# Sparse attention with a feed-forward layer: tile addresses on multiples of 512 bytes, and one place instead of two per attention group

## The chip, the cores and the metric

The kernel runs on one core of a Trainium2 chip. The metric is device time in microseconds (us) of one execution, as the median of several runs. TensorE (PE in the profile) does the matrix products, VectorE (DVE) and ScalarE (ACT) the elementwise work, GpSimd (POOL) a little at the start, and SyncE (SP) issues the transfers.

## What is computed

Attention with two sparse masks over 8 batches of 576 tokens and 8 heads of 64, and a two-layer feed-forward network over the 4608 tokens that it gives. The reference, cut to what matters:

```python
def _attn_ref(q, k, v):                 # q, k, v: (8, 8, 576, 64), float32
    scores = scale * np.matmul(q, k.transpose(0, 1, 3, 2))
    mask_local = (rel >= 0) & (rel < 32)                      # heads 0 to 3
    mask_strided = (rel >= 0) & (pos_k % 32 == pos_q % 32)    # heads 4 to 7
    scores = np.where(masks, scores, -1e9)
    attn = np.exp(scores - np.max(scores, axis=-1, keepdims=True))
    attn = attn / (np.sum(attn, axis=-1, keepdims=True) + 1e-09)
    return np.matmul(attn, v)

def _moe_ref(x, w_in, w_out):           # x: (4608, 512), w_in: (512, 2048)
    h = x @ w_in
    return (h * (1.0 / (1.0 + np.exp(-h)))) @ w_out
```

## The kernel before

**Attention.** A batch is cut into six groups (`GROUPS`, line 77): groups 0 to 2 hold tiles of the local mask, groups 3 to 5 tiles of the strided one. A group `c` of all 48 goes through five steps on TensorE, and each is followed by work elsewhere:

- `scores` (line 348): small products of q and k into a PSUM bank; `peak` (line 358) then masks and finds the maxima on VectorE, and ScalarE takes the exponentials (line 376); `total` (line 391) finishes the sums on VectorE;
- `turn` (line 402): three or four 128x128 transposes of the exponentials (`sm`), and a copy to `pt` on ScalarE (line 410);
- `values` (line 412): small products with v (line 418 for a local group, 426 for a strided one), followed by `share` on VectorE (local) or `sorted` on ScalarE (strided);
- `back` (line 452), for local groups alone: three transposes of `xq` (line 456), and `done` copies them to `xb` on ScalarE.

**Feed-forward.** The tokens are cut into nine blocks of 512, and d_ff into 16 chunks of 128. `hidden` (line 488) is a stretch of 12 matmuls, 128x128 stationary and 512 columns moving: the weights stand in the array, `xhi` or `xlo` moves. `silu` makes `ghi` and `glo` of it on ScalarE and VectorE (lines 498, 502, 510, 514). `output` (line 534) is again a stretch of 12 wide matmuls: `ghi` or `glo` stands in the array and the second layer's weights move. It works one chunk behind, so the order on TensorE is hidden(fc), output(fc - 1), hidden(fc + 1), and so on: two stretches a chunk, 32 a block. Both layers keep a high and a low part of every float32 value, hence three products per term.

**Weights of the second layer.** Chunks 0 to 6 and the low part of 7 and 8 have tiles of their own. The rest is kept in tiles that the start no longer needs (`lent`, line 175): the high parts of chunks 7 and 8 in `kbd2`, the high parts of chunks 9 to 11 in `vbd2`, their low parts in `zeros`, chunks 12 to 15 in `stage0` to `stage3`. All of them are read by TensorE as the moving operand.

**Order.** Block 0 is arranged by a small planner (`Steps`, lines 97 to 159). From block 1 on TensorE's order is written out by hand (lines 745 to 780); the order on the other engines follows from a scheduler, while dependencies decide the waits. While block k runs, the attention of batch k + 1 is done between the stretches: `plan` (line 746) gives each group two places, counted in half chunks. At the first stand `back` of the group before and `values` of the group; three half chunks later `turn` of the next group, `scores` of the one after that and `total`. The PSUM ring `ps` has four banks, which `hidden` and all attention steps share.

Of the kernel before, what the change touches and what calls it, by code (L numbers as in the profile page):

```python
# [13 lines left out]
F32 = mybir.dt.float32  # L14
# [9 lines left out]
B, H, S, D = 8, 8, 576, 64  # L24
# [4 lines left out]
P = 128  # L29
# [3 lines left out]
NFC = DFF // P  # L33
# [11 lines left out]
VT = 12  # L45
KBUFS = 2
VBUFS = 2
# [115 lines left out]
def sparse_attention_ffn(ctx: ExitStack, tc: tile.TileContext, kqt, vt, w_in, w_out, out):  # L163
    nc = tc.nc
    const = ctx.enter_context(tc.tile_pool(name="const", bufs=1))
    io = ctx.enter_context(tc.tile_pool(name="io", bufs=2))
    xp = ctx.enter_context(tc.tile_pool(name="xp", bufs=2))
    att = ctx.enter_context(tc.tile_pool(name="att", bufs=2))
# [10 lines left out]

    kbds = [const.tile([P, 3, QW], F32, name=f"kbd{i}") for i in range(KBUFS + 1)]
    vbds = [const.tile([P, 2, VT * D], F32, name=f"vbd{i}") for i in range(VBUFS + 1)]
    zeros = const.tile([P, VT * D], F32, name="zeros")
    ident = const.tile([P, P], F32, name="ident")

# [12 lines left out]
    vbds = [vbd.rearrange("p h (t d) -> p h t d", d=D) for vbd in vbds]  # L199
# [7 lines left out]
    def keep(m, p0, rows, shape, steps, base, channel):  # L207
        part = m[p0 : p0 + rows, : math.prod(shape)]
        nc.gpsimd.affine_select(
            out=part, in_=part, pattern=[[s, c] for s, c in zip(steps, shape)],  # L210
            base=base, channel_multiplier=channel, compare_op=ALU.is_ge, fill=NEG,
        )
# [15 lines left out]
    for t in range(P // KW):  # L228
        keep(m, t * KW, KW, [4, NJ], [-NJ, -1], 0, 1)
        keep(m, t * KW, KW, [4, NJ], [NJ, 0], NJ - 1, -1)  # L230
    masks[False, ()] = m


    cuts = ((0, NFC), (0, 7, 9, 12, 14, NFC))
# [91 lines left out]
    class Attention:  # L326
# [21 lines left out]
        def scores(self):  # L348
            g, kbd = self.g, self.kbd
            self.pss = self.bank("pss")  # L350
            s_ps = self.pss.rearrange("p (c h k) -> p c h k", h=2, k=KW)
            for t, c, rows in self.tiles:
                nc.tensor.matmul(  # L353
                    s_ps[rows, c], kbd[:, 1, g.q0[t] : g.q0[t] + g.rows],
                    kbd[:, 0:3:2, g.k0[t] : g.k0[t] + KW], start=True, stop=True,
                )

        def peak(self):
            g = self.g
            s_ps = self.pss.rearrange("p (c h k) -> p c h k", h=2, k=KW)  # L360
            self.sm = att.tile([P, 512], F32, name="sm", bufs=3)
            self.s_sb = s_sb = self.sm.rearrange("p (c k h) -> p c h k", h=2, k=KW)
            self.nmax = nmax = att.tile([P, 4, 2], F32, name="nmax", bufs=4)
            self.rsum = rsum = att.tile([P, 4, 2], F32, name="rsum", bufs=4)
            self.inv = rsum[:, : g.n].unsqueeze(3).broadcast_to([P, g.n, 2, KW])
            for c in range(g.n):
                for h in range(2):

                    nc.vector.tensor_tensor_reduce(  # L369
                        out=s_sb[:, c, h], in0=s_ps[:, c, h],  # L370
                        in1=masks[g.local, g.starts[c]][:, :KW],
                        scale=-SCALE, scalar=BIG, op0=ALU.add, op1=ALU.min,
                        accum_out=nmax[:, c, h : h + 1],
                    )
                    if not self.quick:
                        nc.scalar.activation(  # L376
                            out=s_sb[:, c, h], in_=s_sb[:, c, h], func=AF.Exp,
                            bias=nmax[:, c, h : h + 1], scale=-1.0,
                            accum_out=rsum[:, c, h : h + 1],
                        )  # L380
# [10 lines left out]
        def total(self):  # L391
            rsum, s_sb = self.rsum[:, : self.g.n], self.s_sb[:, : self.g.n]
            if self.quick:
                nc.vector.tensor_reduce(out=rsum, in_=s_sb, op=ALU.add, axis=mybir.AxisListType.X)
            nc.vector.tensor_scalar_add(rsum, rsum, 1e-9)
            nc.vector.reciprocal(rsum, rsum)
# [5 lines left out]
        def turn(self):  # L402
            self.psp = self.bank("psp")
            for c in range(self.g.n):
                at = slice(c * P, (c + 1) * P)
                nc.tensor.transpose(self.psp[:, at], self.sm[:, at], ident)  # L406
# [5 lines left out]
        def values(self):  # L412
            g, pt, vbd = self.g, self.pt, self.vbd
            self.pso = pso = self.bank("pso")
            if g.local:
                o_ps = pso.rearrange("p (c h d) -> p c h d", h=2, d=D)
                for t, c, rows in self.tiles:
                    nc.tensor.matmul(  # L418
                        o_ps[rows, c], pt[:, c * P + rows.start : c * P + rows.stop], vbd[:, :, t],
                        start=True, stop=True,  # L420
                    )
                return
            for t, c, rows in self.tiles:
                p0 = c * P + rows.start
                for h in range(2):
                    nc.tensor.matmul(  # L426
                        pso[h * D : (h + 1) * D, t * SEQ : (t + 1) * SEQ], vbd[:, h, t],
                        pt[:, p0 : p0 + SEQ], start=True, stop=True,
                    )
# [22 lines left out]
        def back(self):  # L452
            self.psx = self.bank("psp")
            for c in range(self.g.n):
                at = slice(c * P, (c + 1) * P)
                nc.tensor.transpose(self.psx[:, at], self.xq[:, at], ident)  # L456
# [6 lines left out]
    def new_x():  # L463
        return [ffn.tile([P, NP, T], F32R, name=n, bufs=1) for n in ("xhi", "xlo")]
# [9 lines left out]
    def x_high(k, x, cc, engine="ACT"):  # L474
        for src, to in parts(k, cc):
            copy[engine](out=x[0][:, cc, to], in_=src)

    def x_low(k, x, cc):
        for src, to in parts(k, cc):
            nc.vector.tensor_sub(out=x[1][:, cc, to], in0=src, in1=x[0][:, cc, to].bitcast(F32))  # L480

    def hidden(fc, x, ccs, ph=None):

        if ph is None:
            ph = ps.tile([P, T], F32, name="ps")
        for cc in ccs:
            for n, (wi, xi) in enumerate(((0, 0), (0, 1), (1, 0))):
                nc.tensor.matmul(  # L488
                    ph, weight(0, wi, fc)[:, cc * P : (cc + 1) * P], x[xi][:, cc],
                    start=(cc, n) == (0, 0), stop=(cc, n) == (NP - 1, 2),  # L490
                )
        return ph
# [25 lines left out]
    def silu(k, fc, ph):  # L518
        th = g = None

        step = P if (k, fc) == (NBLK - 1, NFC - 1) else T
        for at in range(0, T, step):
            cols = slice(at, at + step)
            th = tanh(ph, cols, th)
            gate(ph, th, cols)
            g = g_high(th, cols, g)
            g_low(th, g, cols)
        return g

    def output(k, fc, g, po):  # L530
        for tt in range(NTT):
            cols = slice(tt * P, (tt + 1) * P)
            for n, (gi, wi) in enumerate(((0, 0), (0, 1), (1, 0))):
                nc.tensor.matmul(  # L534
                    po[tt], g[gi][:, cols], weight(1, wi, fc),
                    start=fc == 0 and n == 0, stop=fc == NFC - 1 and n == 2,
                )

    def store(k, po):
        for tt in range(NTT):  # L540
            osb = ffn.tile([P, DM], F32, name="osb", bufs=2)
            nc.scalar.mul(out=osb, in_=po[tt], mul=0.5)
            r0 = k * T + tt * P
            nc.sync.dma_start(out=out[r0 : r0 + P, :], in_=osb)
# [197 lines left out]
            groups[c].back()  # L742
            groups[c].done()

    half = 2 * NFC
    plan = collections.defaultdict(list)
    for c in range(2 * NG, len(groups)):
        b, gi = divmod(c, NG)
        at = 2 * NFC * (b - 1) + round(1 + 5.33 * gi)
        plan[at] += [(back, c - 1), (values, c)]  # L750
        plan[at + 3] += [(turn, c + 1), (scores, c + 2), (total, c + 2)]

    def between():
        nonlocal half
        for act, c in plan.pop(half, ()):
            act(c)
        half += 1

    load_due()
    lag = (0, NFC - 1, state["g", NFC - 1])  # L760
# [2 lines left out]
    for k in range(1, NBLK):  # L763
        for fc in range(NFC):
            ph = hidden(fc, x, range(NP))
            new = (k, fc, silu(k, fc, ph))
            if fc == NFC - 1 and k + 1 < NBLK:
                x = new_x()
                for cc in range(NP):
                    x_high(k + 1, x, cc)  # L770
                    x_low(k + 1, x, cc)
            between()
            output(*lag, po)
            if fc == 0:
                store(k - 1, po)
                po = [ps_o.tile([P, DM], F32, name="po") for _ in range(NTT)]
            between()
            lag = new
    output(*lag, po)
    store(NBLK - 1, po)  # L780
# [64 lines left out]
```

## Time and profile before

| | |
|---|---|
| Median of three runs (lowest to highest) | 946.02 us (945.76 to 948.33) |
| The profiled execution | 947.45 us, span 945.7 us |
| Busy share of the span: PE, DVE, ACT, POOL | 98%, 45%, 34%, 2% |
| Mean granted TensorE clock | 0.992 of full speed |
| Chain that ended last | PE 95%, DMA 2%, DVE 1%, ACT 1% |
| Of that chain: output (L534), hidden (L488) | 42%, 42% |

The span runs from the first to the last instruction. The chain is followed back from the last instruction, at each step to what released it; it lies on TensorE almost from end to end. Wide matmuls overlap in the trace: one is shown with 0.39 us, but the next starts some 0.23 us after it. So what a stretch costs is read from the start of its first matmul to the start of what follows.

### The profile page before, as it was taken

What the parts mean: (1) busy time and instruction counts of PE and PEld (TensorE: products, weight loads), DVE (VectorE), ACT (ScalarE), POOL (GpSimd) and SP (SyncE); (2) the same over time, 40 slices, a digit from 0 to 9 for tenths busy, and PEclk for the clock granted to TensorE, in tenths of its full rate; (3) what the DMA queues carried; (4) which work ended last, traced back from release to release, by engine and by line L of the source; (5) the groups of instructions that cost most, each with busy time, mean ns of one, the idle gap of its engine ahead of it and who ended that gap; (6) DMA issues with size and microseconds to landing.
All of it is one profiled execution on the core that took longest, in us unless ns stands there. A gap on an engine that the chain in (4) does not pass through costs nothing.

```text
span 945.7 us, 15110 instructions
## 1 busy us (share of the span) xinstructions
PE 926.4 (98%) x5896; PEld 746.0 (79%) x5896; DVE 426.2 (45%) x1379; ACT 323.5 (34%) x915; POOL 19.1 (2%) x39
## 2 busy tenths in 40 slices
PE   6899999999999999999999999999999999999997
PEld 4687877888788778888788878887788888888886
DVE  7899754343443443443543443424434343333332
ACT  4877633232333242232422342323423131112111
POOL 4001000000000000000000000000000000000000
PEclk9799999999999999999999999999999999999999
DMA  7885512111311122011311121111310010001001
GB/s 234 278 263 191 180 57 86 32 47 36 98 46 39 37 64 84 26 47 52 100 30 35 55 96 36 42 45 36 106 32 10 1 45 1 1 0 45 1 1 45
DMA packets 36487, 62.86 MB, mean 66 GB/s; under 512 B 4160, under 2 KB 23616, under 8 KB 36416
## 3 DMA queue, kind: packets, MB, share of 16 engines
q1 hardware_dynamic: 36416, 61.90, 20.6%
q8 instruction: 46, 0.75, 0.3%
q14 instruction: 25, 0.20, 0.1%
HBM read 52.45 MB, written 9.44 MB: 65 GB/s over the span
## 4 chain that ended last, share of the span: by engine, by line
PE 95%; DMA 2%; DVE 1%; ACT 1%; SPq 0%; issue 0%; ACTq 0%
PE po L534 42%; PE ps L488 42%; PE ps L353 4%; PE ps L426 2%; PE ps L418 2%; PE ps L406 2%; DMA kbd<-kqt 1%; PE ps L456 1%; DMA stage<-w_in 1%; PE po L406 0%; SPq L317 0%; DVE xlo L480 0%; DMA out<-osb 0%; PE po L426 0%; PE po L418 0%
## 5 line engine op out<-in xcount | busy, mean ns | idle before, releaser
L488 PE MATMUL ps<-xhi,w 128*128 128x512 f32 x1152 | 388.0, 396 | 2.0 <-ACT pt L410 2.0
L502 DVE SCALAR_TENSOR_TENSOR th<-th,ps 128x512 f32<-128x512 f32 (+1 forms) x147 | 99.3, 675 | 401.5 <-ACT th L498 401.0
L488 PEld LDWEIGHTS ps<-xhi,w 128*128 128x128 f32 x1152 | 217.1, 188 | 54.1 <-ACT pt L410 4.2
L498 ACT ACTIVATE th<-ps 128x512 f32<-128x512 f32 (+1 forms) x147 | 86.2, 586 | 469.2 <-PE ps L488 467.5
L488 PE MATMUL ps<-xlo,w 128*128 128x512 f32 x576 | 225.7, 392 | 0.1
L534 PE MATMUL po<-w,ghi 128*128 128x512 f32 x576 | 185.7, 393 | 0.0
L488 PEld LDWEIGHTS ps<-xlo,w 128*128 128x128 f32 x576 | 108.8, 189 | 22.8 <-DVE xlo L480 1.3
L534 PEld LDWEIGHTS po<-w,ghi 128*128 128x128 f32 x576 | 106.6, 188 | 25.1 <-issue 3.6
L514 DVE TENSOR_TENSOR glo<-th,ghi 128x512 fp32r<-128x512 f32 (+1 forms) x147 | 100.0, 680 | 9.4 <-ACT ghi L510 0.4
L534 PE MATMUL po<-w,glo 128*128 128x512 f32 x252 | 98.3, 390 | 0.0
L534 PE MATMUL po<-stage,ghi 128*128 128x512 f32 x288 | 89.5, 392 | 0.0
L376 ACT ACTIVATE sm<-sm,nmax 128x64 f32<-128x64 f32 x228 | 76.9, 341 | 25.8 <-DVE nmax L369 25.8
L534 PEld LDWEIGHTS po<-stage,ghi 128*128 128x128 f32 x288 | 53.6, 188 | 11.3
L510 DVE CAST ghi<-th 128x512 fp32r<-128x512 f32 (+1 forms) x138 | 57.9, 420 | 8.5
L353 PE MATMUL ps<-kbd 128*32 128x128 f32 (+1 forms) x928 | 47.8, 292 | 8.7 <-POOL ident masks.py:197 5.2
L534 PE MATMUL po<-stage,glo 128*128 128x512 f32 x144 | 56.1, 390 | 0.0
L534 PEld LDWEIGHTS po<-w,glo 128*128 128x128 f32 x252 | 47.3, 188 | 10.1
L353 PEld LDWEIGHTS ps<-kbd 128*32 128x32 f32 (+1 forms) x928 | 35.0, 125 | 18.5 <-issue 9.4
L534 PE MATMUL po<-vbd,ghi 128*128 128x512 f32 x108 | 43.9, 407 | 0.0
L534 PE MATMUL po<-vbd,glo 128*128 128x512 f32 x108 | 42.6, 395 | 0.0
L376 ACT ACTIVATION_READ_ACCUMULATOR sm<-sm,nmax 128x1 f32 x228 | 42.6, 187 | 0.0
L534 PE MATMUL po<-zeros,ghi 128*128 128x512 f32 x108 | 42.5, 393 | 0.0
(81 smaller groups left out, 736.1 us busy)
## 6 DMA issues: line engine op xcount, KB each, us to landing
vbd<-vt SPq DMA_DIRECT2D x48, 192.0 KB, 2.9
out<-osb SPq DMA_DIRECT2D x36, 256.0 KB, 2.1
stage<-w_in SPq DMA_DIRECT2D x16, 512.0 KB, 4.6
stage<-w_out SPq DMA_DIRECT2D x16, 512.0 KB, 4.6
kbd<-kqt SPq DMA_DIRECT2D x32, 221.0 KB, 3.0
kbd<-kqt SPq DMA_DIRECT2D x32, 208.0 KB, 3.0
vbd<-vt SPq DMA_DIRECT2D x32, 128.0 KB, 2.5
kbd<-kqt SPq DMA_DIRECT2D x16, 224.0 KB, 3.2
```

Of the source, the lines that this page charges most:

```text
L353: nc.tensor.matmul(s_ps[rows, c], kbd[:, 1, g.q0[t] : g.q0[t] + g.rows], kbd[:, 0:3:2, g.k0[t] : g.k0[t] + KW], start=True, stop=True,)
L376: nc.scalar.activation(out=s_sb[:, c, h], in_=s_sb[:, c, h], func=AF.Exp, bias=nmax[:, c, h : h + 1], scale=-1.0, accum_out=rsum[:, c, h : ...
L406: nc.tensor.transpose(self.psp[:, at], self.sm[:, at], ident)
L418: nc.tensor.matmul(o_ps[rows, c], pt[:, c * P + rows.start : c * P + rows.stop], vbd[:, :, t], start=True, stop=True,)
L426: nc.tensor.matmul(pso[h * D : (h + 1) * D, t * SEQ : (t + 1) * SEQ], vbd[:, h, t], pt[:, p0 : p0 + SEQ], start=True, stop=True,)
L456: nc.tensor.transpose(self.psx[:, at], self.xq[:, at], ident)
L488: nc.tensor.matmul(ph, weight(0, wi, fc)[:, cc * P : (cc + 1) * P], x[xi][:, cc], start=(cc, n) == (0, 0), stop=(cc, n) == (NP - 1, 2),)
L498: nc.scalar.activation(out=th[:, cols], in_=ph[:, cols], func=AF.Tanh, scale=0.5)
L502: nc.vector.scalar_tensor_tensor(out=th[:, cols], in0=th[:, cols], scalar=1.0, in1=ph[:, cols], op0=ALU.add, op1=ALU.mult,)
L510: copy[engine](out=g[0][:, cols], in_=th[:, cols])
L514: nc.vector.tensor_sub(out=g[1][:, cols], in0=th[:, cols], in1=g[0][:, cols].bitcast(F32))
L534: nc.tensor.matmul(po[tt], g[gi][:, cols], weight(1, wi, fc), start=fc == 0 and n == 0, stop=fc == NFC - 1 and n == 2,)
```

## The change

First, some small filler tiles and another order of the first tiles shift the tiles' addresses, and the maxima and sums of a group move into one tile (`sums`). Each partition's address of a tile, as what is left after multiples of 512 bytes:

| tile | before | after |
|---|---|---|
| `kbd2`, `kbd0` | 128 | 0 |
| `kbd1` | 384 | 256 |
| `vbd0` to `vbd2`, `zeros`, `ident` | 384 | 0 |
| `stage0` to `stage3`, the weights' own tiles, `xb`, `sm` | 0 | 0 |
| `xhi`, `xlo`, `ghi`, `glo`, `th`, `pt`, `xq`, `osb` | 256 | 0 |

Second, from block 1 on (the second of the nine) each group has one place in a block instead of two: behind `output` of chunks 0, 3, 5, 8, 11 and 13, in front of the next `hidden`. There stand, in this order, `turn` of the next group, `back` of the group before, `scores` of the group after next, `values` of the group, and `total`.

```diff
+    const.tile([P, 96], F32, name="pad0")
+    vbds = [const.tile([P, 2, VT * D], F32, name=f"vbd{i}") for i in range(VBUFS + 1)]
     kbds = [const.tile([P, 3, QW], F32, name=f"kbd{i}") for i in range(KBUFS + 1)]
-    vbds = [const.tile([P, 2, VT * D], F32, name=f"vbd{i}") for i in range(VBUFS + 1)]
+    const.tile([P, 64], F32, name="pad1")
     zeros = const.tile([P, VT * D], F32, name="zeros")
...
     masks[False, ()] = m
+    const.tile([P, 96], F32, name="pad3")
...
-            self.nmax = nmax = att.tile([P, 4, 2], F32, name="nmax", bufs=4)
-            self.rsum = rsum = att.tile([P, 4, 2], F32, name="rsum", bufs=4)
+            sums = att.tile([P, 4, 4, 2], F32, name="sums", bufs=4)
+            self.nmax, self.rsum = nmax, rsum = sums[:, 0], sums[:, 1]
...
-    half = 2 * NFC
-    plan = collections.defaultdict(list)
+    plan = {}
     for c in range(2 * NG, len(groups)):
         b, gi = divmod(c, NG)
-        at = 2 * NFC * (b - 1) + round(1 + 5.33 * gi)
-        plan[at] += [(back, c - 1), (values, c)]
-        plan[at + 3] += [(turn, c + 1), (scores, c + 2), (total, c + 2)]
-
-    def between():
-        nonlocal half
-        for act, c in plan.pop(half, ()):
-            act(c)
-        half += 1
+        plan[b - 1, (0, 3, 5, 8, 11, 13)[gi]] = c
+
+    def between(k, fc):
+        if (k, fc) in plan:
+            c = plan[k, fc]
+            turn(c + 1)
+            back(c - 1)
+            scores(c + 2)
+            values(c)
+            total(c + 2)
...
-            between()
             output(*lag, po)
             if fc == 0:
                 store(k - 1, po)
                 po = [ps_o.tile([P, DM], F32, name="po") for _ in range(NTT)]
-            between()
+            between(k, fc)
             lag = new
```

TensorE in block 1 before, the first place of group 13 (the second of its batch), between a hidden stretch and an output stretch (the number behind a tile's name is the program's, x12 counts equal instructions):

```order
L488 MATMUL ps<-xlo,w_0_451 128x512
L488 MATMUL ps<-xhi,w_0_466 128x512
L456 MATMUL ps<-ident,xq 128x128 x3
L418 MATMUL ps<-vbd_80,pt 32x128 x12
L534 MATMUL po<-w_0_540,ghi 128x512
```

The second place of the same group, three half chunks on, between an output stretch and a hidden stretch:

```order
L534 MATMUL po<-w_0_540,glo 128x512
L406 MATMUL ps<-ident,sm 128x128 x3
L353 MATMUL ps<-kbd_77 64x128 x8
L488 MATMUL ps<-xhi,w_0_451 128x512
L488 MATMUL ps<-xlo,w_0_451 128x512
```

The same group's one place in the changed kernel, whose line numbers are three or four higher:

```order
L538 MATMUL po<-w_0_537,glo 128x512
L410 MATMUL ps<-ident,sm 128x128 x3
L460 MATMUL ps<-ident,xq 128x128 x3
L357 MATMUL ps<-kbd_81 64x128 x8
L422 MATMUL ps<-vbd_78,pt 32x128 x12
L492 MATMUL ps<-xhi,w_0_448 128x512
```

The four steps now follow each other directly, with one return to the wide matmuls instead of two. The number of instructions is the same on every engine, and block 0's order is the same too, except for the names of the tiles.

ScalarE around the same two places before (in between, `L498` is tanh of a chunk):

```order
L461 COPY xb<-ps 128x384
L498 ACTIVATE th<-ps 128x512
L410 COPY pt<-ps 128x384
L376 ACTIVATE sm,rsum<-sm,nmax 128x64 x8
L498 ACTIVATE th<-ps 128x512 x2
```

And around the one place of the changed kernel:

```order
L502 ACTIVATE th<-ps 128x512 x3
L414 COPY pt<-ps 128x384
L465 COPY xb<-ps 128x384
L380 ACTIVATE sm,sums<-sm,sums 128x64 x8
L502 ACTIVATE th<-ps 128x512 x2
```

Both copies and the eight exponentials now stand in a row in front of one tanh.

## Rows read from the trace of the kernel before

**Rows 1.** The page's first part: busy us, share of the span, instructions.

```profile
PE 926.4 (98%) x5896; PEld 746.0 (79%) x5896; DVE 426.2 (45%) x1379; ACT 323.5 (34%) x915; POOL 19.1 (2%) x39
```

**Rows 2.** The longest of PE's waits: total us, times, longest.

```profile
PE ps L353 <- POOL ident masks.py:197: 5.2, 1, 5.2
```

**Rows 3.** Windows, blocks 3, 7, 8: length, busy PE, PEld, DVE, ACT, POOL, clock, DMA.

```profile
348.78:452.72 103.94, 103.94 (x694) 83.58 (x690) 42.40 (x155) 34.59 (x121) 0.00 (x0) 1.00 0.18 54
...
762.34:850.12 87.78, 87.73 (x385) 71.94 (x384) 31.41 (x56) 14.41 (x26) 0.00 (x0) 1.00 0.03 13
850.12:937.60 87.48, 87.48 (x385) 72.00 (x384) 31.26 (x58) 12.63 (x24) 0.00 (x0) 1.00 0.03 13
```

**Rows 4.** Timeline of PE, block 3, two attention places: start us, us, instruction.

```profile
351.63 0.61 PE L534 MATMUL po<-stage,ghi 128*128 128x512 f32 x2
...
354.44 0.86 PE L418 MATMUL ps<-vbd,pt 128*32 128x128 f32 x24
355.23 0.50 PE L488 MATMUL ps<-xhi,w 128*128 128x512 f32 x1
...
358.10 0.62 PE L534 MATMUL po<-w,ghi 128*128 128x512 f32 x2
...
360.82 0.39 PE L488 MATMUL ps<-xhi,w 128*128 128x512 f32 x1
...
363.54 0.49 PE L406 MATMUL ps<-ident,sm 128*128 128x128 f32 x3
363.96 0.86 PE L353 MATMUL ps<-kbd 128*32 128x128 f32 x24
364.76 0.73 PE L534 MATMUL po<-w,ghi 128*128 128x512 f32 x2
...
367.61 0.39 PE L488 MATMUL ps<-xhi,w 128*128 128x512 f32 x1
```

**Rows 5.** Timeline of PE, block 3: a turn with four transposes.

```profile
399.11 0.60 PE L406 MATMUL ps<-ident,sm 128*128 128x128 f32 x4
399.64 1.09 PE L353 MATMUL ps<-kbd 128*64 128x128 f32 x16
```

**Rows 6.** Timeline of PE, block 0: scores followed directly by values; back followed by values.

```profile
62.33 0.86 PE L353 MATMUL ps<-kbd 128*32 128x128 f32 x24
63.01 0.84 PE L418 MATMUL ps<-vbd,pt 128*32 128x128 f32 x24
63.78 0.73 PE L534 MATMUL po<-w,ghi 128*128 128x512 f32 x2
...
87.48 0.55 PE L456 MATMUL ps<-ident,xq 128*128 128x128 f32 x3
87.95 0.86 PE L418 MATMUL ps<-vbd,pt 128*32 128x128 f32 x24
```

**Rows 7.** Timeline of PE, block 8 (no attention): chunks 7 to 10, first matmul of each stretch.

```profile
896.41 0.40 PE L534 MATMUL po<-kbd,ghi 128*128 128x512 f32 x1
...
899.15 0.40 PE L488 MATMUL ps<-xhi,w 128*128 128x512 f32 x1
...
904.66 0.40 PE L488 MATMUL ps<-xhi,w 128*128 128x512 f32 x1
...
907.42 0.40 PE L534 MATMUL po<-vbd,ghi 128*128 128x512 f32 x1
...
910.21 0.39 PE L488 MATMUL ps<-xhi,w 128*128 128x512 f32 x1
...
912.95 0.40 PE L534 MATMUL po<-vbd,ghi 128*128 128x512 f32 x1
```

**Rows 8.** The page's groups: tanh and gate of a chunk, exponentials of a group.

```profile
L502 DVE SCALAR_TENSOR_TENSOR th<-th,ps 128x512 f32<-128x512 f32 (+1 forms) x147 | 99.3, 675 | 401.5 <-ACT th L498 401.0
...
L498 ACT ACTIVATE th<-ps 128x512 f32<-128x512 f32 (+1 forms) x147 | 86.2, 586 | 469.2 <-PE ps L488 467.5
...
L376 ACT ACTIVATE sm<-sm,nmax 128x64 f32<-128x64 f32 x228 | 76.9, 341 | 25.8 <-DVE nmax L369 25.8
```

## The prediction
> **What bounds the kernel.** I read the page's busy shares first, then TensorE's waits, then windows of whole blocks, and last the timeline of TensorE, stretch by stretch. TensorE is busy for 98% of the span, the next engine for 45% [rows 1]. Its longest single wait is 5.2 us, and it lies at the start, before the identity matrix is ready [rows 2]. From block 1 on it never stands still: block 3 takes 103.94 us and TensorE is busy for 103.94 of them, at the full clock, which is 2.4 GHz [rows 3]. So the time is the sum of what stands in TensorE's queue, and a change saves exactly what it takes out of that sum, while work on other engines counts only if it becomes late.
>
> What is in the sum beside the bare products shows in the timeline. A stretch of 12 wide matmuls that stands between two others takes 2.72 us: the output stretch from 358.10 to 360.82, and the hidden one from 360.82 to 363.54 [rows 4]. A block has 32 of them, 87.04 us. Block 8, which has no attention beside it, takes 87.48 us [rows 3], so 0.44 us there is neither attention nor bare stretch. Block 3 takes 16.90 us more than 87.04, for the small products and for going to them and back.
>
> **Going there and back.** After a visit to the small products, the next wide stretch is longer. Behind scores it takes 364.76 to 367.61, 2.85 us, 0.13 more than bare; behind values 355.23 to 358.10, 2.87 us, 0.15 more [rows 4]. In front of a visit it depends on what opens it. Before transposes the wide stretch keeps its 2.72 us (360.82 to 363.54), before values it takes 2.81 us (351.63 to 354.44), 0.09 more [rows 4]. A full attention block now has 12 visits, six that end with scores and six that end with values. Three of the latter also open with values, since strided groups have no `back`. The change leaves six visits, all opening with `turn` and ending with values.
> - Returns: six of 0.13 us go, 0.78 us a block. Block 6 has no scores for its last two groups and makes 11 returns; five go, 0.65 us.
> - Openings: three of 0.09 us go, 0.27 us a block.
> - Blocks 1 to 5 together 5 x 1.05, block 6 0.92: **6.2 us**.
>
> **Steps that now touch.** `back` follows `turn` at once in 18 places (three groups in each of six blocks). Three transposes take 0.42 us up to the next step (363.54 to 363.96), four take 0.53 (399.11 to 399.64) [rows 4, 5]; so a further one is 0.11, and three further ones cost 0.32 instead of 0.42. I take 0.10 us each, **1.8 us**. The trace has no six in a row. The other end is three transposes behind another small step, in block 0, which took 0.47 us (87.48 to 87.95) [rows 6]: a loss of 0.05 each, 0.9 us.
>
> Values follow scores at once in 34 places. Scores take 0.80 us when a wide stretch follows (363.96 to 364.76) [rows 4] but 0.68 us when values follow (62.33 to 63.01), and those values then take 0.77 us [rows 6], against 0.79 in 354.44 to 355.23 [rows 4]. I take 0.11 us for each place, **3.7 us**. That row is of two local steps; places with a strided step have no row of their own. A strided scores step ends with other tile sizes, so the bounds are nothing and 0.13 us, 0 to 4.4 us.
>
> **Addresses.** In block 8 nothing but wide stretches runs, and yet they differ. The output of chunk 7, two thirds of whose moving weights lie in `kbd2` (128 bytes past a multiple of 512), takes 896.41 to 899.15, 2.74 us. The output of chunk 9, all of whose moving weights lie in `vbd2` and `zeros` (384 past), takes 907.42 to 910.21, 2.79 us [rows 7]. The hidden stretches right behind such outputs are longer as well, 2.76 us (904.66 to 907.42) and 2.74 (910.21 to 912.95) [rows 7], although their own operands lie as those of the other chunks do; they seem to work off a delay. Two outputs at 0.03, three at 0.07, two hidden stretches at 0.04 and three at 0.02 give 0.41 us, near the 0.44 that block 8 has over its bare stretches. Hidden moves `xhi` and `xlo` at 256 past and still takes 2.72, so 256 is harmless and the further shift of x, g and the rest to 0 brings nothing. All nine blocks run these outputs: 9 x 0.4, **3.6 us**. The lower end is nothing, if the cause is not the start address.
>
> **The step that loses.** At a block's end ScalarE and VectorE make the next block's `xhi` and `xlo`, which must wait for the last hidden stretch and are needed by the first hidden one of the next block. Only one output stretch lies between, and before the change a visit with `turn` and `scores` as well, 1.2 us (as from 363.54 to 364.76) [rows 4]. Its place moves to chunk 13. Block 7 already opens without such a visit, and takes 87.78 us against 87.48 in block 8 [rows 3], whose x comes in fewer pieces: 0.30 us for x that is late. Five more block starts (2 to 6) lose that cover: **1.5 us lost**. Ends: nothing, if the rest of ScalarE's queue is shorter by then, and twice as much.
>
> **At nothing.** The merged `sums` tile, the fillers and the moved loads cost nothing: each load stands two or three chunks ahead of its reader, 10.9 us or more at 5.44 us a chunk, beside DMA that is 18% busy in block 3 [rows 3].
>
> **Sum.** 6.2 + 1.8 + 3.7 + 3.6 - 1.5 = 13.8 us. Against the profiled execution (947.45 us, span 945.7) that is 933.7 us. Its duration is 1.4 us above the median of the runs, so against the median, 946.02, I predict **932.2 us**.
>
> **Rivals.**
> 1. *The addresses do nothing.* The slow stretches share low addresses and their lent tiles as much as their start, and the delay that spreads into hidden stretches is odd for a mere start. Then 932.2 + 3.6 = 935.8 us. The Trainium skill ("SBUF — State Buffer", Specifications (TRN2)) speaks for this: its lines are 16 bytes, and a penalty falls on crossing into a new line, so starts of 128 and 384, all multiples of 16, would be alike. By that rule the time is this rival's; the trace does not bear it out as it stands, since chunk 9's output is 0.07 us above a bare one. Chance 0.18.
> 2. *Touching steps do not shorten.* If the saving in block 0 is peculiar to two local steps, the 3.7 us go and `back` loses 0.9 instead of gaining 1.8: 932.2 + 6.4 = 938.6 us. Chance 0.09.
> 3. *Equal starts collide, and it is slower.* After the change what stands in the array and what moves past it start at the same place of 512 bytes in every wide matmul; before they were 128 or 256 apart. If that cost as much as the worst stretch now, (2.79 - 2.72) / 12 = 5.8 ns each [rows 7], the 9 x 32 x 12 = 3456 wide matmuls would lose 20 us against a gain of 10.2 without addresses: 956 us. It decides the sign from 2.9 ns on. No row shows such a pair, and 0 against 256 gives the same 2.72 whichever of the two moves. Chance 0.05.
> 4. *Gates come late.* A visit now puts both copies and all exponentials in front of the next tanh. With `turn`, `back` and eight exponentials (0.34 us each [rows 8]) ScalarE is free some 4.9 us after the visit began, while the next hidden stretch ends at about 5.4. tanh and gate take 0.59 and 0.68 us [rows 8], and the two steps after it about as much; their output stretch begins two stretches later, 5.4 us on. So some 3 us are spare, and the four banks of `ps` are free too, the oldest by the gate of the chunk before. To eat the gain, each of 36 visits would have to be 3.4 us later: 946 us, no change. Chance 0.05.
>
> The forecast, with its own bounds, has 0.60. The last 0.03 is for a gain beyond it: bare stretches that get below 2.72 us once everything lies at 0, for which nothing in the rows speaks.
>
> **Range and chances.** The upper end is rival 2 with twice the loss at block starts, 938.6 + 1.5, or 940.1 us; the lower is the forecast with all of the touching steps (0.7 more) and no late x (1.5 more), 930.0. With half a microsecond for the spread of the runs: 929.5 to 940.6 us. What a measurement can tell here is about 0.3%, 2.8 us. The forecast, rivals 1 and 2 and the rest are all faster by more than that, 0.90; rival 4 is mostly within it, 0.05; rival 3 is slower, 0.05.
>
> **What would show it.** Bare output stretches of chunks 9 to 11 at 2.72 us instead of 2.79 show the addresses right, with hidden stretches behind them at 2.72; 2.79 again shows rival 1. Full attention blocks of about 101.8 us instead of 103.94 show the sum of the moved part and the addresses; block 8 of 87.1 the addresses alone. Scores before values at 0.68 us in a local place, and six transposes in 0.74, show the touching steps. TensorE idle in the first hidden stretch of blocks 2 to 6, by about 0.3 us, shows the late x. Bare stretches above 2.72 everywhere would be rival 3, and idle time of TensorE released by VectorE's `glo` or ScalarE's copies behind the visits rival 4.

## The result and the profile after

The changed kernel takes 934.72 us in the median of four runs (932.88 to 937.39), the kernel before 946.01 us (945.76 to 948.33). The ratio is 0.9885, with a 95% interval from 0.9866 to 0.9904: 11.3 us less, which is small but clear of the scatter. The forecast was 932.2 us, between 929.5 and 940.6. The profiled execution took 937.39 us with a span of 935.6 us, 10.1 us less than the profiled one before.

The page's first part answers to [rows 1], and its chain still lies almost wholly on TensorE, with 3% on VectorE that was 1% before:

```profile
PE 916.1 (98%) x5896; PEld 747.7 (80%) x5896; DVE 431.8 (46%) x1379; ACT 322.6 (34%) x915; POOL 19.0 (2%) x39
...
PE 91%; DVE 3%; DMA 3%; ACT 2%; issue 0%; SPq 0%; ACTq 0%
```

TensorE has 10.3 us less work by the profile, with as many instructions. The windows of blocks 3, 7 and 8, cut as in [rows 3] (length, busy PE, PEld, DVE, ACT, POOL, clock, DMA):

```profile
345.64:447.94 102.30, 102.25 (x690) 83.81 (x689) 43.29 (x155) 34.60 (x122) 0.00 (x0) 1.00 0.18 55
752.95:840.39 87.44, 87.39 (x386) 71.95 (x384) 31.43 (x56) 14.41 (x26) 0.00 (x0) 1.00 0.03 13
840.39:927.53 87.14, 87.14 (x386) 72.02 (x384) 31.26 (x58) 12.52 (x24) 0.00 (x0) 1.00 0.03 13
```

A full attention block went from 103.94 to 102.30 us, where the forecast had 101.8; block 8 from 87.48 to 87.14, near the forecast 87.1. New in the first row are 0.05 us in which TensorE is idle. VectorE is busy for 0.9 us more with the same instructions; that is off the path, and its cause stays open.

The timeline of TensorE at the opening of block 3 and at its first visits (start us, us, instruction) shows every step of the forecast, and the one that failed. (The chunks 0, 3, 5 and so on of the change count the passes of the loop: the output that stands there is the one of the chunk before, so at the opening of a block it is chunk 15 of the block before, which reads `stage`.)

```profile
345.64 0.39 PE L492 MATMUL ps<-xhi,w 128*128 128x512 f32 x1
...
346.77 0.61 PE L492 MATMUL ps<-xhi,w 128*128 128x512 f32 x2
347.44 0.50 PE L492 MATMUL ps<-xlo,w 128*128 128x512 f32 x1
...
348.71 0.39 PE L538 MATMUL po<-stage,ghi 128*128 128x512 f32 x1
```

```profile
351.43 0.49 PE L410 MATMUL ps<-ident,sm 128*128 128x128 f32 x3
351.85 0.86 PE L357 MATMUL ps<-kbd 128*32 128x128 f32 x24
352.53 0.84 PE L422 MATMUL ps<-vbd,pt 128*32 128x128 f32 x24
353.30 0.50 PE L492 MATMUL ps<-xhi,w 128*128 128x512 f32 x1
...
369.78 0.49 PE L410 MATMUL ps<-ident,sm 128*128 128x128 f32 x3
370.11 0.49 PE L460 MATMUL ps<-ident,xq 128*128 128x128 f32 x3
370.53 1.09 PE L357 MATMUL ps<-kbd 128*64 128x128 f32 x16
371.55 0.86 PE L422 MATMUL ps<-vbd,pt 128*32 128x128 f32 x24
372.34 0.50 PE L492 MATMUL ps<-xhi,w 128*128 128x512 f32 x1
...
403.37 0.88 PE L357 MATMUL ps<-kbd 128*64 128x128 f32 x12
404.08 1.09 PE L430 MATMUL ps<-pt,vbd 128*64 128x54 f32 x32
```

- The first hidden stretch now takes 345.64 to 348.71, 3.07 us: the matmul that reads `xlo` of the third quarter comes late (two matmuls at 346.77 reach to 347.44 instead of 347.22). That is the forecast loss, 0.35 us a block start over the bare 2.72 where 0.30 was forecast.
- `turn` in front of `back` takes 0.33 us (369.78 to 370.11) instead of 0.42: three touching transposes save 0.1 us, as forecast.
- Two local steps: scores take 0.68 us (351.85 to 352.53) and values 0.77, as in [rows 6]. Two strided ones save as well: these 12 scores take 0.71 us (403.37 to 404.08), where the trace of before has 0.81 for them (312.76 to 313.57). But strided scores in front of local values take 1.02 us (370.53 to 371.55), and those values 0.79 (371.55 to 372.34): nothing saved. Four of the six places in a block are mixed pairs, two of this kind and two with local scores in front of strided values, which save nothing either.

### The profile page after: what moved, and what is told of

Same layout as the page of the kernel before. It is cut to its first block, busy times and chain, and to the rows that moved or that the text cites. A ratio compares the mean times of both kernels' runs of the same rounds, so it can differ in the third digit from the quotient of the medians.

```text
span 935.6 us, 15127 instructions
## 1 busy us (share of the span) xinstructions
PE 916.1 (98%) x5896; PEld 747.7 (80%) x5896; DVE 431.8 (46%) x1379; ACT 322.6 (34%) x915; POOL 19.0 (2%) x39
## 4 chain that ended last, share of the span: by engine, by line
PE 91%; DVE 3%; DMA 3%; ACT 2%; issue 0%; SPq 0%; ACTq 0%
PE ps L492 41%; PE po L538 39%; PE ps L357 4%; PE ps L430 2%; PE ps L422 2%; DMA kbd<-kqt 2%; PE ps L410 2%; DVE xlo L484 1%; DMA stage<-w_in 1%; PE ps L460 1%; DVE glo L518 1%; ACT th L502 0%; ACT xhi L480 0%; DVE ghi L514 0%; ACT stage L256 0%
## 5 line engine op out<-in xcount | busy, mean ns | idle before, releaser
L538 PE MATMUL po<-w,ghi 128*128 128x512 f32 x576 | 183.5, 390 | 0.4 <-DVE ghi L514 0.4
L380 ACT ACTIVATE sm<-sm,sums 128x64 f32<-128x64 f32 x228 | 76.8, 341 | 17.3 <-DVE sums L373 17.3
L514 DVE CAST ghi<-th 128x512 fp32r<-128x512 f32 (+1 forms) x138 | 58.1, 421 | 11.3 <-PE po L538 0.5
L414 ACT COPY pt<-ps 128x384 f32<-128x384 f32 (+1 forms) x42 | 21.6, 513 | 79.4 <-PE ps L410 79.4
L380 ACT ACTIVATION_READ_ACCUMULATOR sm<-sm,sums 128x1 f32 x228 | 42.9, 188 | 0.0
L373 DVE CUSTOM_DVE_ANT_0 sm<-ps,mask_strided 128x64 f32<-128x64 f32 x176 | 27.3, 220 | 33.3 <-PE ps L357 33.3
```

Of the source, the lines that this page charges most:

```text
L373: nc.vector.tensor_tensor_reduce(out=s_sb[:, c, h], in0=s_ps[:, c, h], in1=masks[g.local, g.starts[c]][:, :KW], scale=-SCALE, scalar=BIG, ...
L380: nc.scalar.activation(out=s_sb[:, c, h], in_=s_sb[:, c, h], func=AF.Exp, bias=nmax[:, c, h : h + 1], scale=-1.0, accum_out=rsum[:, c, h : ...
L414: nc.scalar.copy(out=self.pt[:, : self.cols], in_=self.psp[:, : self.cols])
L514: copy[engine](out=g[0][:, cols], in_=th[:, cols])
L538: nc.tensor.matmul(po[tt], g[gi][:, cols], weight(1, wi, fc), start=fc == 0 and n == 0, stop=fc == NFC - 1 and n == 2,)
```

## The experiments

All runs are compared with runs of the kernel before on the same chip. Totals scatter by some 2 to 5 us between executions, so beside each total stands the length of block 3, and of block 8 where it matters, cut from the first hidden matmul to the next block's; in these, blocks 2 to 5 of one execution agree within 0.05 us.

### The addresses alone (e1)

The kernel before with the first part of the change (its last filler, `pad3`, belongs to it too):

```diff
+    const.tile([P, 96], F32, name="pad0")
+    vbds = [const.tile([P, 2, VT * D], F32, name=f"vbd{i}") for i in range(VBUFS + 1)]
     kbds = [const.tile([P, 3, QW], F32, name=f"kbd{i}") for i in range(KBUFS + 1)]
-    vbds = [const.tile([P, 2, VT * D], F32, name=f"vbd{i}") for i in range(VBUFS + 1)]
+    const.tile([P, 64], F32, name="pad1")
...
+            sums = att.tile([P, 4, 4, 2], F32, name="sums", bufs=4)
+            self.nmax, self.rsum = nmax, rsum = sums[:, 0], sums[:, 1]
```

> Only the tiles' addresses (and the merged sums tile) change, the order stays that of the kernel before. Theory (the start address of the moving operand costs): the outputs of chunks 7 to 11 fall from 2.75 and 2.79 to 2.72 us, the hidden stretches behind them too, a full attention block from 103.94 to about 103.54, block 8 from 87.48 to about 87.14; in all 3.6 us less, about 942.4 us. Rival (the slow stretches came from the order of the work, or from low addresses as such): 2.75 and 2.79 stay, 946 us.

Measured: 942.25 us (941.36 to 943.09), ratio 0.9967, interval 0.9954 to 0.998. The windows of blocks 3 and 8 of this run:

```profile
346.22:449.88 103.66, 103.66 (x693) 83.56 (x689) 42.41 (x155) 34.62 (x121) 0.00 (x0) 1.00 0.18 54
846.10:933.24 87.14, 87.14 (x385) 72.00 (x384) 31.27 (x58) 12.51 (x24) 0.00 (x0) 1.00 0.03 13
```

The output of chunk 9 in block 8 and the hidden stretch behind it, first matmul of each:

```profile
903.32 0.39 PE L537 MATMUL po<-vbd,ghi 128*128 128x512 f32 x1
...
906.04 0.39 PE L491 MATMUL ps<-xhi,w 128*128 128x512 f32 x1
```

Block 8 does what was expected, block 3 falls by 0.28 us instead of 0.40. That the order of the work made those stretches slow is out: the order is that of before, and the bare outputs of chunks 7 to 11 in block 8 take 2.72 us each in this trace (chunk 9 from 903.32 to 906.04, where it took 2.79). In an attention block a part of the address delay had been hidden in the returns: the output of chunk 9, behind a visit there, took 2.89 us before and takes 2.85 to 2.86 here, 0.03 to 0.04 less and not 0.07.

### The order alone (e2)

The changed kernel with the tile statements of the kernel before (the diff above, undone).

> Only the order changes, the tiles lie where they lay before. Theory (two parts that add up): outputs of chunks 7 to 11 at 2.75 and 2.79 us again, a full attention block at 102.30 + 0.40 = 102.70 us, in all about 938.3 us. Rival (the addresses also shorten the small products, or the returns): the block is at 103.0 or more, 940 us and above.

Measured: 938.08 us (936.57 to 939.75), ratio 0.9927, interval 0.9913 to 0.9942.

```profile
342.70:445.35 102.65, 102.60 (x691) 83.81 (x689) 43.29 (x155) 34.63 (x122) 0.00 (x0) 1.00 0.18 55
839.22:926.71 87.49, 87.49 (x386) 72.01 (x384) 31.27 (x58) 12.52 (x24) 0.00 (x0) 1.00 0.03 13
```

As the theory says: block 3 at 102.65, block 8 back at 87.49. The rival is out: each small step of block 3 takes what it takes in the changed kernel, to 0.01 us. The order alone takes 1.29 us out of an attention block, the addresses alone 0.28, both together 1.64: they add up, with 0.07 us more than the sum. In the new order no visit stands in front of an output, so no return hides the address delay of one; that this is the whole 0.07 is not shown. Against the 945.07 us that the kernel before took beside them on the same chip, the totals of e1 and e2 save 2.8 and 7.0 us.

### Which start costs (e3)

The changed kernel with its lent tiles shifted by other fillers:

```diff
-    const.tile([P, 96], F32, name="pad0")
+    const.tile([P, 16], F32, name="pad0")
     vbds = [const.tile([P, 2, VT * D], F32, name=f"vbd{i}") for i in range(VBUFS + 1)]
-    kbds = [const.tile([P, 3, QW], F32, name=f"kbd{i}") for i in range(KBUFS + 1)]
-    const.tile([P, 64], F32, name="pad1")
     zeros = const.tile([P, VT * D], F32, name="zeros")
+    kbds = [const.tile([P, 3, QW], F32, name=f"kbd{i}") for i in range(KBUFS)]
+    const.tile([P, 32], F32, name="pad1")
+    kbds.append(const.tile([P, 3, QW], F32, name=f"kbd{KBUFS}"))
...
-    const.tile([P, 96], F32, name="pad3")
...
+            if i < LENT:
+                const.tile([P, (24, 24, 40, 24)[i]], F32, name=f"pads{i}")
             stage = const.tile([P, 512, 2], I32, name=f"stage{i % AHEAD}")
+            if i == LENT - 1:
+                const.tile([P, 96], F32, name="pads_end")
```

> The changed kernel with its lent tiles at other starts, counted from a multiple of 512 bytes: high parts of chunks 7 and 8 at 320, chunks 9 to 11 at 192, chunks 12 and 13 at 288 (high) and 32 (low), chunks 14 and 15 at 384 (high) and 128 (low); the rest stays at 0. Theory A (only multiples of 256 are free): outputs of 9 to 15 all at 2.79 us, of 7 and 8 at 2.75. Theory B (odd multiples of 128 cost, others do not): only chunks 14 and 15 at 2.79, the rest at 2.72. Rival C (low addresses are slow, whatever the start): chunks 7 to 11 slow, 12 to 15 at 2.72. A gives about 941 us, B 937, C 938.

Measured: 942.97 us (939.74 to 945.21), ratio 0.9971, interval 0.9954 to 0.9988. The timeline of block 8, first matmuls of outputs 7, 9, 12 and 14 and of the stretches behind them (behind output 14 it is output 15):

```profile
892.66 0.40 PE L542 MATMUL po<-kbd,ghi 128*128 128x512 f32 x1
...
895.46 0.40 PE L496 MATMUL ps<-xhi,w 128*128 128x512 f32 x1
...
903.77 0.39 PE L542 MATMUL po<-vbd,ghi 128*128 128x512 f32 x1
...
906.57 0.39 PE L496 MATMUL ps<-xhi,w 128*128 128x512 f32 x1
...
920.39 0.63 PE L542 MATMUL po<-stage,ghi 128*128 128x512 f32 x2
...
923.19 0.40 PE L496 MATMUL ps<-xhi,w 128*128 128x512 f32 x1
...
931.51 0.62 PE L542 MATMUL po<-stage,ghi 128*128 128x512 f32 x2
...
934.30 0.63 PE L542 MATMUL po<-stage,ghi 128*128 128x512 f32 x2
```

Starts of 192 (903.77 to 906.57), of 288 and 32 (920.39 to 923.19), and of 384 and 128 (931.51 to 934.30) take 2.79 to 2.80 us, and the two thirds at 320 take 2.80 as well (892.66 to 895.46), where two thirds at 128 took 2.74 [rows 7]. So theory A holds in its rule: every start tried off a multiple of 256 costs, and 0 and 256 do not. Its size for chunks 7 and 8, 2.75 us, was too small: eight matmuls of twelve at 320 cost as much as twelve at 192, while eight at 128 cost about a quarter of that, so the price is not one figure for each matmul. The `stage` tiles lie higher than `kbd2` and are as slow once shifted, so the place in memory (rival C) is out.

Block 8 takes 88.01 us here against 87.14. From block 1 on the profile takes 5.9 us more than the changed kernel's, near the 6.3 that theory A's 941 stands for. The median of the runs lies 2 us above 941; some of it is the start of the execution, which reached block 1 0.8 us later in this profile than in the changed kernel's.

The fillers also shifted what the expectation takes to stay at 0: by their sizes `ident` starts at 64, `kbd0` at 192, `kbd1` at 448, `vbd0` and `vbd1` at 192. Block 8 reads none of them, and the small products of block 3, which do, take the same as in the changed kernel to 0.01 us.

The Trainium skill ("SBUF — State Buffer", Specifications (TRN2)) gives lines of 16 bytes with a penalty for crossing into a new one, by which all the starts here, multiples of 32, would be alike. They are not: 2.80 us for these against 2.72 at 0.

### The late x (e4 and e6)

What VectorE does in the changed kernel at the opening of block 3, where `xlo` is made in eight pieces, two for each quarter of x:

```profile
345.36 1.02 DVE L484 TENSOR_TENSOR xlo<-xb,xhi 128x192 fp32r<-128x192 f32 x3
346.30 0.69 DVE L518 TENSOR_TENSOR glo<-th,ghi 128x512 fp32r<-128x512 f32 x1
346.90 1.16 DVE L484 TENSOR_TENSOR xlo<-xb,xhi 128x320 fp32r<-128x320 f32 x3
```

The second piece of the third quarter stands behind glo, at 346.90, and the matmul that reads it starts at 347.44. In e4 VectorE makes six of the eight pieces before the last chunk's ghi, and the other two before its glo:

```diff
-            new = (k, fc, silu(k, fc, ph))
             if fc == NFC - 1 and k + 1 < NBLK:
-                x = new_x()
-                for cc in range(NP):
-                    x_high(k + 1, x, cc)
-                    x_low(k + 1, x, cc)
+                with tc.manual_schedule(engines={mybir.EngineType.DVE}):
+                    th = tanh(ph)
+                    gate(ph, th)
+                    x = new_x()
+                    for cc in range(NP):
+                        x_high(k + 1, x, cc)
+                        x_low(k + 1, x, cc)
+                        if cc == 2:
+                            g = g_high(th)
+                    g_low(th, g)
+                new = (k, fc, g)
+            else:
+                new = (k, fc, silu(k, fc, ph))
```

> The changed kernel, but at a block's end VectorE makes the low parts of the next block's x before ghi and glo of the last chunk (ghi stands before the last quarter of x, glo behind it). Theory (the first hidden stretch of blocks 2 to 7 waits for VectorE's xlo, behind glo): it takes 2.72 to 2.76 us instead of 3.07, six times 0.3 is 1.9 us less, about 932.8 us. Rival (ScalarE's xhi sets the pace): 3.07 stays, 934.7 us. Second rival (glo of the last chunk becomes late instead): the hidden stretch is short, and TensorE idles about as long in the output stretch behind it.

Measured: 932.65 us (932.17 to 935.19), ratio to the kernel before 0.9872, interval 0.9856 to 0.9888. Blocks 3 and 8, the opening of block 3, and VectorE in front of it:

```profile
342.31:444.26 101.95, 101.95 (x691) 83.94 (x689) 43.29 (x155) 34.59 (x122) 0.00 (x0) 1.00 0.18 55
835.27:922.31 87.04, 87.04 (x385) 72.10 (x384) 31.28 (x59) 12.63 (x24) 0.00 (x0) 1.00 0.03 13
```

```profile
342.31 0.39 PE L492 MATMUL ps<-xhi,w 128*128 128x512 f32 x1
...
345.03 0.61 PE L538 MATMUL po<-stage,ghi 128*128 128x512 f32 x2
```

```profile
341.02 2.10 DVE L484 TENSOR_TENSOR xlo<-xb,xhi 128x192 fp32r<-128x192 f32 x6
...
343.37 0.75 DVE L484 TENSOR_TENSOR xlo<-xb,xhi 128x192 fp32r<-128x192 f32 x2
```

The first hidden stretch takes 2.72 us, and block 3 loses 0.35 us. Both rivals are out: ScalarE was quick enough, and glo is in time. Block 8 is now 87.04 us, exactly 32 bare stretches of 2.72.

In e6 a visit stands in front of the first hidden stretch again:

```diff
-        plan[b - 1, (0, 3, 5, 8, 11, 13)[gi]] = c
+        at = (b - 1, (0, 3, 5, 8, 11, 13)[gi])
+        plan[(b - 2, NFC - 1) if gi == 0 and b > 2 else at] = c
```

> The changed kernel with the first group's place of blocks 2 to 6 moved from behind chunk 0 to behind chunk 15 of the block before, just in front of the next block's first hidden stretch. Theory (that stretch waits 0.35 us for x because nothing stands before it): it takes 2.85 to 2.88 us like any stretch behind a visit, and hidden of chunk 1 takes 2.72 instead of 2.88; five block starts save 0.35 us each, 1.7 us, about 933.0 us. Rival (ScalarE and VectorE, which make x then, delay the visit's own steps or the next gates): the wait comes back as idle time of TensorE in that visit or behind it, 934.7 us or more.

Measured: 932.79 us (931.84 to 933.35), ratio 0.9861, interval 0.9833 to 0.9889.

```profile
343.39:445.35 101.96, 101.96 (x694) 83.93 (x690) 43.20 (x155) 34.81 (x121) 0.00 (x0) 1.00 0.18 55
```

The same 0.35 us a block, by cover instead of by order; TensorE is busy throughout, so the rival is out. Both cures give what the theory says, so the cause is shown: x is late because VectorE works through the last chunk's ghi and glo before the last pieces of `xlo`, and before the change a visit of 1.2 us stood over it.

### Pairs of one kind (e5), and steps taken apart (e7)

e5 takes the groups in turn, local and strided, so that scores and values in a place are of one kind:

```diff
-GROUPS += [Group(False, 8 * i, n) for i, n in enumerate((8, 8, 6))]
+STRIDED = [Group(False, 8 * i, n) for i, n in enumerate((8, 8, 6))]
+GROUPS = [g for pair in zip(GROUPS, STRIDED) for g in pair]
...
-    done = (outs[:2], outs[1:3], outs[3:5], outs[4:6])
+    done = (outs[0:4:2], outs[2:6:2], outs[1:5:2], outs[3:6:2])
```

> The changed kernel with the six groups of a batch taken in turn, local, strided, local and so on, so that scores of the group after next and values of the group are always of one kind; before, two of six places had that. Theory (scores and values shorten each other only where both use tiles of the same width: 0.135 us for two local steps, 0.15 for two strided ones, nothing for a mixed pair): all six places save, a full attention block falls from 102.30 to about 101.73 us, in all 3.3 us less, about 931.4 us (the planner of block 0 also sees another order, which may move its end by a microsecond or two). Rival (the two short pairs are short for their place in the block or their sizes): mixed or not, four places stay as they are, 102.3 us.

Measured: 932.44 us (931.59 to 933.35), ratio 0.9855, interval 0.9831 to 0.988. Block 3, and a strided place in it:

```profile
343.50:445.21 101.71, 101.65 (x690) 83.95 (x689) 43.16 (x155) 34.43 (x122) 0.00 (x0) 1.00 0.18 55
```

```profile
368.46 1.10 PE L358 MATMUL ps<-kbd 128*64 128x128 f32 x16
369.38 1.09 PE L431 MATMUL ps<-pt,vbd 128*64 128x54 f32 x32
370.41 0.49 PE L493 MATMUL ps<-xhi,w 128*128 128x512 f32 x1
```

Block 3 falls by 0.59 us, the theory's 0.57. The same 16 score products that took 1.02 us in front of local values take 0.92 us in front of strided ones, and 32 strided values 1.03 instead of the 1.07 behind local scores (422.78 to 423.85 in the changed kernel). So it is the kind that decides, not the place. Local steps use tiles 32 wide and strided ones 64, so the runs do not part the width from the rest of the kind. The total is 1 us above the 931.4 that was expected.

e7 puts `back` between scores and values:

```diff
             turn(c + 1)
-            back(c - 1)
             scores(c + 2)
+            back(c - 1)
             values(c)
```

> The changed kernel with back moved between scores and values, so that turn and back no longer touch, nor scores and values in the three places that have a back. Theory: turn goes from 0.33 or 0.44 to 0.42 or 0.53 us in three places, and the one place with two strided steps loses its 0.15; a full attention block rises from 102.30 to about 102.75 us. Rival (the order inside a visit is indifferent, what counts is the one return): 102.30 us.

Measured: 938.91 us, in a single run, so that the length of the block is what counts here.

```profile
344.67:447.62 102.95, 102.90 (x690) 83.74 (x689) 43.44 (x155) 34.56 (x122) 0.00 (x0) 1.00 0.18 54
```

```profile
369.25 1.10 PE L357 MATMUL ps<-kbd 128*64 128x128 f32 x16
370.28 0.55 PE L460 MATMUL ps<-ident,xq 128*128 128x128 f32 x3
370.76 0.86 PE L422 MATMUL ps<-vbd,pt 128*32 128x128 f32 x24
```

The block rises by 0.65 us instead of 0.45. The rival (only the return counts) is out. The miss is `back` behind scores, 0.48 us (370.28 to 370.76) instead of the 0.42 that I had put down, three times: the row for it stood in [rows 6].

### The two together (e8)

e4's and e5's edits in one kernel.

> The interleaved groups together with x before ghi and glo at a block's end (e4 and e5 in one). Theory: the parts lie in different stretches and add up, a full attention block at 101.73 - 0.35 = 101.4 us, block 8 at 87.04 us (32 bare stretches), in all about 929.4 us. Rival (one gain eats the other, or a step becomes late): more than 931 us.

Measured: 930.72 us (928.72 to 931.24), ratio to the kernel before 0.9833, interval 0.9808 to 0.9859.

```profile
342.88:444.26 101.38, 101.38 (x690) 84.09 (x689) 43.19 (x155) 34.43 (x122) 0.00 (x0) 1.00 0.18 55
833.57:920.61 87.04, 87.04 (x386) 72.07 (x384) 31.26 (x58) 12.62 (x24) 0.00 (x0) 1.00 0.03 13
```

Block 3 is at the expected 101.4 us, block 8 at 87.04: the parts add up. The total is 1.3 us above the expected 929.4, just short of the rival's 931; block 1, which opens behind a block 0 of another order, takes 101.88 us (139.62 to 241.50), 0.5 more than the blocks behind it. By its median this is the fastest of the kernels run, 4.0 us below the changed kernel's; the two were not timed side by side, and the kernel before took 946.17 us beside the one and 946.01 beside the other.

## Why the prediction was right, and where its sum was off

The direction, the mechanism and the range were right; the sum was 2.5 us too hopeful against the median, and one of its terms was mis-sized by most of that. The total alone would not have shown the mechanism: rival 1's 935.8 us lies nearer to the measured 934.72 than the forecast's 932.2, and it is the blocks and the experiments that rule it out. The parts can now be set against the trace. From the first hidden matmul of block 1 to the last output of block 8 the profile lost 10.4 us (796.7 to 786.3), where the terms for that part said 13.4, with 3.2 of the 3.6 for the addresses.
- **Going there and back**, 6.2 us: right. The order alone took 1.29 us out of a block (e2); without the 0.29 of touching transposes and the 0.28 of touching pairs, and with the 0.35 of late x put back, 1.07 is left for returns and openings, against 1.05. Over all of e2's trace from block 1 on, which is 7.6 us shorter than the one before, 6.0 us are left for them in the same way.
- **`back` behind `turn`**, 1.8 us: right, 18 times 0.095 is 1.7. e7 shows it from the other side.
- **Values behind scores**, 3.7 us: this term was mis-sized. I carried 0.11 us, taken from a local pair, over to all 34 places, and named the bound of nothing for strided steps without weighing it. The rows quoted there give 0.14 for that pair (0.12 on the scores, 0.02 on the values), so the upper bound of 0.13 was too low as well. And the trace of before had a warning: the 16 strided scores in front of the `back` of [rows 6] took 1.03 us (86.45 to 87.48), no less than the 1.02 in front of a wide stretch (380.28 to 381.30), so a small step behind does not shorten by itself. Measured are 0.135 us for a local pair, 0.15 for a strided pair and nothing for a mixed one, twelve places in all: 1.7 us. The 2.0 us that are missing are most of the gap. e5 shows the rule.
- **Addresses**, 3.6 us: the cause was right (e1, e3) and the size too large for attention blocks. I took block 8's 0.4 us for all nine blocks; in an attention block of the order before, returns hid a part, and 0.28 was left. For blocks 1 to 8 that gives 6 x 0.28 + 2 x 0.34 = 2.4 us instead of 3.2.
- **The step that loses**, 1.5 us: right in its place, 0.35 instead of 0.30 a block, 1.75 us, because the opening of block 8, from which I took the difference, is itself a little late (2.76 us, not 2.72).
- **At nothing**: right from block 1 on, where no wait of TensorE on a load or a late gate shows. Three waits that were not there or shorter before lie in block 0 (total us, times, longest), whose order is the same:

```profile
PE po L460 <- DVE xq L440: 1.2, 1, 1.2
PE po L538 <- DVE glo L518: 0.5, 1, 0.5
PE po L538 <- DVE ghi L514: 0.4, 1, 0.4
```

  All the waits of TensorE that the profile lists lie in block 0; they come to 14.0 us here and 13.9 before, since others became shorter. This profile reached block 1 at 141.23 us and the one before at 140.86, although bare outputs of chunks 9 and 11 in block 0 take 2.72 us instead of 2.78 to 2.79; the last section comes back to it.

With the measured sizes the sum is 6.3 + 1.7 + 1.7 + 2.4 - 1.75 = 10.4 us, which is what the trace shows. The 6.3 is block 3's 1.07 carried over to the six blocks; the two parts alone, 7.6 us by the trace of e2 and 2.4 by that of e1, come to 10.0, and the rest is saved only by both together.

Of the rivals, the first fell with e1 and e3. The second came true in part: mixed pairs save nothing, but strided pairs do, and `back` gains. The third did not come: with everything at 0 a bare stretch takes 2.72 us as before, so neither a collision nor a gain beyond the forecast is there. The fourth did not come in these blocks.

## What to carry to other kernels

When one engine is busy for all of a stretch, add up its queue by kinds of transition, not by instructions alone: what a step costs depends on what stands before and behind it, and a pair of steps is worth only what a row of that very pair shows. Put the moving operand of wide float32 matmuls at multiples of 256 bytes; the loss is small (up to 3% of a stretch), and a few filler tiles remove it. Before moving work away, ask what it covered: here 1.2 us of small products had hidden a late operand, and reordering VectorE's queue at that point brought it back.

## What the runs showed of the hardware

- A wide float32 matmul whose moving operand starts off a multiple of 256 bytes is slower by some 6 ns (2.79 to 2.80 us for 12 instead of 2.72), for starts at 192, at 384, at 288 with 32 and at 384 with 128, and the delay runs on into the following matmuls, whose operands lie well: 2.74 to 2.76 us for the next stretch. Where only eight of twelve start off, it was 2.74 us at 128 and 2.80 at 320. What inside the chip does it stays open.
- A change between small products of one width (128*32 or 128*64 in the rows) costs 0.1 to 0.15 us less than one between two widths or to the wide matmuls. That it is the width which does it is not shown apart from the kind of group.
- The profiles differ in the start. In the first 60 us the mean granted clock was 0.89 of full speed in the changed kernel's profile and 1.00 in e2's, and TensorE reached block 1 at 141.23 and at 137.59 us. The windows of the first 60 us of these two:

```profile
0.00:60.00 60.00, 46.80 (x448) 36.59 (x449) 48.25 (x183) 41.65 (x73) 12.51 (x33) 0.89 0.81 266
```

```profile
0.00:60.00 60.00, 44.79 (x492) 34.39 (x496) 49.77 (x186) 42.99 (x77) 12.56 (x33) 1.00 0.84 271
```

  Both have the same order of work there. All ten profiles at hand reach block 1 between 137.4 and 142.0 us, which is as wide as the scatter of the totals. The later starts go with the lower clock: of the eight with this order in block 0, the three at 0.89 reach block 1 at 140.86 to 141.99 us, the five at 0.94 to 1.00 at 137.44 to 138.94. Whether the clock alone accounts for it was not tried.
